# PSUM banks and transpose order at the head of a transformer block, and the order of its last K group

## The chip, the core and the metric

The kernel runs on one core of a Trainium2 chip. The metric is the device time of one execution in microseconds. A core has TensorE (PE in the profile; PEld is its weight load), VectorE (DVE), ScalarE (ACT), GpSimd (POOL) and SyncE (SP), which here only issues transfers.

## The reference

A DiT block with adaptive layer norm, 2 x 256 tokens, width 1152, two heads of 576, all in bf16:

```python
mod = (_silu(c) @ w_mod).reshape(B, 6, 1, D)
shift_a, scale_a, gate_a, shift_m, scale_m, gate_m = [mod[:, i] for i in range(6)]
h = _layernorm(x, axis=-1) * (1 + scale_a) + shift_a
qkv = (h @ wqkv).reshape(B, N, 3, H, Dh)
# ... softmax(q k^T) v, @ wo ...
x = x + gate_a * a
h2 = _layernorm(x, axis=-1) * (1 + scale_m) + shift_m
m = _gelu(h2 @ w_fc1) @ w_fc2
return x + gate_m * m
```

## The kernel before

The kernel is written as a list of units with their reads and writes. A helper orders them, works out who must wait for whom (in PSUM by whole bank, so that a matmul into a bank waits for every reader of that bank) and emits the waits. TensorE executes its units in program order. `S.first` fixes the order of the first units of the other engines.

At the head, four tiles of 128 tokens are normalised (`xn_t`), transposed on TensorE into PSUM (`xn_T`), and scaled by 1 + scale_a on the way out (`hk`). The scale itself is built by small two-column matmuls (`sca`) whose weights arrive by transfer, three k-tiles at a time. K (`k_first`, `k_pair`) is accumulated k-tile by k-tile as the weights arrive (a k-tile is 128 of the 1152 rows that are summed over). While TensorE has nothing to do, it runs filler matmuls (`warm`), so that its clock is up when the work starts.

```python
        XB = [(4, 5, 3), (6, 2, 7)]

        def xslot(b, kt, n=256):
            return ps16(XB[b][kt // 4], (kt % 4) * 256 + (512 if kt == 8 and b == 1 else 0), n)
# ...
        def hk(kt, b, eng="dve"):
            dst = HK[:, kt, b * 256:(b + 1) * 256]
            s1 = ps32(1 if kt == 0 else 7, 2 * kt, 1) if kt % KC == 0 and b == 0 else SC1A[:, kt * 2 + b:kt * 2 + b + 1]
            src = xslot(b, kt) if kt < KC else HX[:, kt, b * 256:(b + 1) * 256]
            if eng == "act":
                act(c_act(256, 1), lambda e: e.activation(out=dst, in_=src, func=ACTF.Copy, scale=s1), [src, s1], [dst], "hk_%d_%d" % (kt, b))
                return
            dve(345 if kt < KC else 285, lambda e: e.tensor_scalar(out=dst, in0=src, scalar1=s1, scalar2=None, op0=ALU.mult),
                [src, s1], [dst], "hk_%d_%d" % (kt, b))

# ...
        KB = [(0, 1, 5, 3), (4, 2, 6)]
        ev_rr = [0]
# ...
        S.unit("pe", 30.0, "ones_f0")
        mm(ps32(1, 0, 2), IDENT, ONES[:, 0:2], True, True)
        sc_ones(1, KC)
        warm(7, "b")
        for n, behind in ((1, "bn_ln1_1_1"), (1, "aggr_ln1_1"), (2, "veps_ln1_1"), (2, "rstd_ln1_1"), (1, "bn_ln1_2_1"), (2, "bn_ln1_2_2")):
            warm(n, behind, behind)
        sca(0, 3)
        xn_T(1)
        sca(3, 6)
        xn_T(0)
        sca(6, 9)
        xn_T(2, 0, 8)
        hk(0, 0)
        sc1a(0, 1, 1)
        sc1a(1, KC)
        hk(1, 0)
        xn_T_copy(0, 4, 8, "act")
        xn_T_copy(0, 8, 9, "act")
        xn_T_copy(0, 3, 4, "act")
        hk(2, 0, "act")

        def k_first(kt):
            for i in range(4):
                k_pair((kt,), i, 0)

        k_first(0)
        k_first(1)
        xn_T(2, 8, 9)
        xn_T(3)
        xn_T_copy(1, 4, 8, "act")
        xn_T_copy(1, 8, 9, "act")
```

(`XB` are the banks of the transposes of tiles 0 and 1, then 2 and 3; `KB` those of K's pairs for the two batches.)

At the end of the K stage the shift rows (`shr`) are computed in row form, cast by DVE, transposed back (`shT`), and added to h (`hx`), from which Q is projected:

```python
        k_pair(range(KT - 2), 3, 1, bank=1)
        k_pair(range(KT - 2, KT), 3, 1, bank=1)
        for k0 in range(0, KT, 3):
            S.unit("pe", 3 * c_mm(CH) + 50.0, "shr_%d" % k0)
            for kt in range(k0, k0 + 3):
                for j, (f0, f1) in enumerate(sh_split):
                    mm(psum[32 * j:32 * j + 2, 0:(f1 - f0) * 128], ST[:, kt:18:9], WSH[:, kt, f0 * 128:f1 * 128],
                       kt == 0, kt == KT - 1, tile_position=(0, 32 * j))
        copy_on("dve", SHR[0:98, :], psum[0:98, 0:CH], CH, False, "shr_ev")
        k17(0, KC, KT)
        k17(1, 0, 1)
        S.unit("pe", KT * 27.0, "shT")
        for j, (f0, f1) in enumerate(sh_split):
            for f in range(f0, f1):
                mm(ps32(0, f * 2, 2), SHR[0:98, (f - f0) * 128:(f - f0 + 1) * 128], IDENT[0:98, 32 * j:32 * j + 2], f == 0, f == KT - 1,
                   skip_group_check=True)
        k17(1, 1, KT)
```

## Time and profile before

| | |
|---|---|
| median of 3 runs before the prediction | 244.41 us (244.25 to 244.98) |
| busy: TensorE, DVE, ACT, GpSimd | 98%, 50%, 28%, 9% |
| fillers at the head (128x512 matmuls) | 5 and 16 |
| K's first matmul, K's k-tile 2, Q's first matmul | 11.07, 13.57, 33.08 us |

To read it: busy time counts a filler like any other matmul, so 98% says that TensorE sets the end, not that it does useful work all the time. The idle time ahead of a group, in square brackets, is given with what released it. The page and its views merge instructions; where I give times to a hundredth of one instruction, they are of the records in the trace that these views are made of. Q's first matmul has no record in this trace (some matmul records are missing); its 33.08 is inferred from its neighbours. The lines themselves stand in the prediction.

### The profile page before, as it was taken

The numbers are of one execution on the slowest core, as the hardware profiler recorded it, in microseconds if no ns is written. First come the engines' busy times: TensorE is split into PE (matmuls) and PEld (weight loads), VectorE is DVE, ScalarE is ACT, GpSimd is POOL, SyncE is SP. The second block draws the span as 40 slices with busy tenths as digits, with TensorE's granted clock in tenths as the row PEclk, the third lists the DMA queues.
The fourth block names the chain that finished last, engine by engine and source line by source line (L and its number), as shares of the span: only waits on it lengthen the run. The fifth ranks groups of instructions, "written<-read, shape, count | busy, mean of one in ns | idle before, by whom it ended". The sixth has DMA issues, their size and how long they took to land.

```text
span 243.1 us, 4000 instructions
## 1 busy us (share of the span) xinstructions
PE 238.2 (98%) x1719; PEld 146.4 (60%) x1728; DVE 120.5 (50%) x219; ACT 67.0 (28%) x136; POOL 21.2 (9%) x39
## 2 busy tenths in 40 slices
PE   7999999999999999999999999999999999999995
PEld 2688854556667666898444444444666566665664
DVE  3833379596988799689999500000022211111112
ACT  4820440355424106973233222223000000000000
POOL 1500000000021186400000000020000000000000
PEclk9999999999999999999999999999999999999999
DMA  6999999999995999999953498002000000000000
GB/s 233 330 362 388 390 391 390 397 413 406 392 357 168 355 389 391 391 311 392 311 170 78 145 329 302 0 24 77 0 16 19 16 16 19 16 16 29 22 16 18
DMA packets 31196, 51.58 MB, mean 212 GB/s; under 512 B 1479, under 2 KB 16843, under 8 KB 31179
## 3 DMA queue, kind: packets, MB, share of 16 engines
q1 hardware_dynamic: 30736, 50.14, 58.3%
q0 software_dynamic: 416, 1.19, 1.5%
q8 instruction: 13, 0.21, 0.4%
q14 instruction: 4, 0.03, 0.0%
q10 hardware_dynamic: 27, 0.00, 0.0%
HBM read 50.14 MB, written 1.19 MB: 211 GB/s over the span
## 4 chain that ended last, share of the span: by engine, by line
PE 98%; DVE 1%; issue 0%; POOL 0%; POOLq 0%
PE psum L688 96%; PE psum L691 2%; DVE arena L972 0%; POOL arena L713 0%; DVE arena L1296 0%; DVE arena L1297 0%; POOL arena L712 0%; DVE arena L963 0%; POOL arena L717 0%; POOLq L1358 0%
## 5 line engine op out<-in xcount | busy, mean ns | idle before, releaser
L688 PE MATMUL psum<-arena 128*128 128x384 bf16 (+9 forms) x1630 | 235.0, 310 | 2.0 <-POOL arena L717 1.4
L688 PEld LDWEIGHTS psum<-arena 128*128 128x128 bf16 (+1 forms) x1639 | 141.2, 97 | 92.0 <-issue 4.1
L1088 DVE SCALAR_TENSOR_TENSOR arena<-arena 128x1152 f32<-128x1152 bf16 x32 | 44.7, 1414 | 0.6
L1296 DVE TENSOR_TENSOR arena<-psum,arena 128x384 f32<-128x384 f32 (+2 forms) x13 | 6.8, 527 | 68.3 <-PE psum L688 68.3
L1204 ACT ACTIVATE arena<-psum 128x512 bf16<-128x512 f32 (+1 forms) x44 | 22.4, 520 | 42.7 <-PE psum L688 42.7
L683 ACT ACTIVATE arena<-psum 128x512 bf16<-128x512 f32 (+6 forms) x38 | 19.9, 546 | 41.0 <-PE psum L688 39.6
L685 DVE CAST arena<-psum 128x512 bf16<-128x512 f32 (+3 forms) x13 | 8.2, 640 | 9.5 <-PE psum L688 9.5
L669 POOL DMA_DIRECT2D dit_scratch<-arena x3 | 1.8, 617 | 116.2 <-DVE arena L685 59.4
L1172 POOL TENSOR_TENSOR arena<-arena 128x384 f32<-128x384 f32 x12 | 10.9, 912 | 10.6 <-DVE arena L1171 9.0
L1115 DVE CAST arena<-psum 72x32 bf16<-72x32 f32 x1 | 0.2, 186 | 21.3 <-PE psum L688 21.3
L741 DVE BATCH_NORM_STATS2 arena<-arena 128x6 f32<-128x384 f32 (+1 forms) x18 | 9.4, 550 | 0.3 <-DMA arena<-in_x_dram 0.2
L1177 ACT ACTIVATE arena<-arena 128x1152 bf16<-128x1152 f32 x4 | 5.3, 1344 | 11.5 <-DVE arena L1176 11.5
L1171 DVE TENSOR_TENSOR arena<-psum,arena 128x384 f32<-128x384 f32 x12 | 6.5, 549 | 1.4 <-PE psum L688 1.4
L1297 DVE TENSOR_TENSOR arena<-arena 128x384 bf16<-128x384 f32 (+2 forms) x13 | 6.8, 527 | 0.5
L691 PE MATMUL psum<-arena 128*128 128x128 bf16 (+1 forms) x89 | 7.1, 219 | 0.0
L691 PEld LDWEIGHTS psum<-arena 128*128 128x128 bf16 (+1 forms) x89 | 5.7, 98 | 1.8 <-DMA arena<-in_c_dram 0.8
L1194 ACT ACTIVATE arena<-psum,arena 128x128 bf16<-128x128 bf16 x16 | 6.0, 456 | 1.3 <-PE psum L691 0.7
L1191 DVE TENSOR_SCALAR arena<-psum,arena 128x128 bf16<-128x128 bf16 x20 | 5.4, 335 | 1.9 <-PE psum L691 1.9
L1092 DVE STREAM_TRANSPOSE arena<-arena 128x1152 f32<-128x1152 f32 x4 | 5.5, 1370 | 0.0
L1095 DVE TENSOR_REDUCE arena<-arena 128x36 f32<-128x1152 f32 x4 | 5.4, 1346 | 0.0
L1018 ACT ACTIVATE arena<-psum,arena 128x256 bf16<-128x256 f32 x8 | 3.7, 472 | 1.3 <-PE psum L688 0.9
L745 POOL TENSOR_TENSOR arena<-arena 128x1 f32<-128x1 f32 x6 | 3.7, 619 | 1.6 <-DVE arena L744 1.6
(48 smaller groups left out, 44.8 us busy)
## 6 DMA issues: line engine op xcount, KB each, us to landing
arena<-in_w_fc_dram SPq DMA_DIRECT2D x9, 1152.0 KB, 7.1
arena<-in_w_fc_dram SPq DMA_DIRECT2D x4, 2592.0 KB, 17.2
arena<-in_w_mod_dram SPq DMA_DIRECT2D x18, 288.0 KB, 8.7
arena<-in_wqkv_dram SPq DMA_DIRECT2D x18, 288.0 KB, 8.7
arena<-in_w_mod_dram SPq DMA_DIRECT2D x3, 1728.0 KB, 20.1
arena<-in_w_mod_dram SPq DMA_DIRECT2D x3, 864.0 KB, 12.0
arena<-in_wqkv_dram SPq DMA_DIRECT2D x1, 2592.0 KB, 17.4
arena<-in_wo_dram SPq DMA_DIRECT2D x1, 2592.0 KB, 24.7
```

Source lines behind the costliest of these rows:

```text
L683: act(c_act(n), lambda e: e.activation(out=dst, in_=src, func=ACTF.Copy), [src], [dst], name)
L685: dve(c_dve_psum16(n) if psum16 else c_dve_psum32(n), lambda e: e.tensor_copy(dst, src), [src], [dst], name)
L688: S.instr(lambda e: e.matmul(o, lhsT=l, rhs=r, start=st, stop=sp, **kw), reads=[l, r], writes=[o])
L691: S.instr(lambda e: e.transpose(o, i_, idn), reads=[i_, idn], writes=[o])
L741: dve(550, lambda e, s=s, o=o: e.bn_stats(out=o, in_=s), [s], [o], "bn_%s_%d" % (tag, ci))
L1088: dve(1270, lambda e, w=w, s=s, acc=acc: e.scalar_tensor_tensor(out=acc, in0=w, scalar=s, in1=acc, op0=ALU.mult, op1=ALU.add), [w, s, acc] ...
L1171: dve(550, lambda e, o=o, ga=ga, x1c=x1c: e.tensor_tensor(out=x1c, in0=o, in1=ga, op=ALU.mult), [o, ga], [x1c], "wo_t1_%d_%d" % (t, ci))
L1172: S.op("pool", 930, lambda e, xs=xs, x1c=x1c: e.tensor_tensor(out=x1c, in0=x1c, in1=xs, op=ALU.add), reads=[x1c, xs], writes=[x1c], name=" ...
L1194: act(440, lambda e, o=o, dst=dst, s1=s1, s2=s2: e.activation(out=dst, in_=o, func=ACTF.Identity, scale=s1, bias=s2), [o, s1, s2], [dst], ...
L1204: act(c_act(ntok), lambda e: e.activation(out=dst, in_=o, func=ACTF.Gelu_apprx_tanh), [o], [dst], "gelu_%d_%d" % (f, tok0))
L1296: dve(c_dve_psum32(w), lambda e, o=o, gm=gm, t1=t1: e.tensor_tensor(out=t1, in0=o, in1=gm, op=ALU.mult), [o, gm], [t1], "fc2_t1_%d_%d" % ( ...
L1297: dve(c_dve_32(w), lambda e, t1=t1, x1c=x1c, ost=ost: e.tensor_tensor(out=ost, in0=t1, in1=x1c, op=ALU.add), [t1, x1c], [ost], "fc2_out_%d ...
```

## The change

The intent: let K start earlier. Tile 1 is normalised before DVE finishes tile 2's statistics; tile 0's last five transposes lie behind the last scale sums, where TensorE used to run transposes of tile 2; tiles 2 and 3 follow K's second k-tile; K's first batch gets banks that ACT isn't still reading; and two small groups change places at the end of the K stage. The diff, in full but for one hunk of DVE, ACT and GpSimd order lists that follows from the rest:

```diff
--- before.py
+++ after.py
@@ -722,7 +722,7 @@
         for i in range(5):
             S.unit("pe", 430.0, "warm_a%d" % i)
             mm(ps32(5), IDENT, Q4B, True, True)
-        CT_PS = ps16(6, 0, 18)
+        CT_PS = ps16(4, 0, 18)
         S.unit("pe", 100, "c_T")
         tr(CT_PS, CSB[0:18, :], IDENT[0:18, 0:18])
         act(200, lambda e: e.activation(out=TH, in_=CT_PS, func=ACTF.Tanh, scale=0.5), [CT_PS], [TH], "c_tanh")
@@ -764,7 +764,7 @@
                 [xt, m, rs], [xn], "xn_%d" % t)
 
 
-        XB = [(4, 5, 3), (6, 2, 7)]
+        XB = [(4, 5, 3), (3, 5, 7)]
 
         def xslot(b, kt, n=256):
             return ps16(XB[b][kt // 4], (kt % 4) * 256 + (512 if kt == 8 and b == 1 else 0), n)
@@ -799,7 +799,7 @@
 
         def hk(kt, b, eng="dve"):
             dst = HK[:, kt, b * 256:(b + 1) * 256]
-            s1 = ps32(1 if kt == 0 else 7, 2 * kt, 1) if kt % KC == 0 and b == 0 else SC1A[:, kt * 2 + b:kt * 2 + b + 1]
+            s1 = ps32(6 if kt == 0 else 7, 2 * kt, 1) if (kt % KC == 0 or kt == 1) and b == 0 else SC1A[:, kt * 2 + b:kt * 2 + b + 1]
             src = xslot(b, kt) if kt < KC else HX[:, kt, b * 256:(b + 1) * 256]
             if eng == "act":
                 act(c_act(256, 1), lambda e: e.activation(out=dst, in_=src, func=ACTF.Copy, scale=s1), [src, s1], [dst], "hk_%d_%d" % (kt, b))
@@ -813,7 +813,7 @@
                 mm(ps32(bank, half * 256, 256), WK[:, kt, j * 128:(j + 1) * 128], HK[:, kt, b * 256:(b + 1) * 256], kt == 0 and half == 0,
                    kt == KT - 1, skip_group_check=True)
 
-        KB = [(0, 1, 5, 3), (4, 2, 6)]
+        KB = [(0, 1, 2, 6), (4, 5, 3)]
         ev_rr = [0]
 
         def k_pair(kts, i, b, bank=None):
@@ -834,7 +834,7 @@
 
         def mod_f0(kt):
             S.unit("pe", 27.0, "sca0_%d" % kt)
-            mm(ps32(1, 0, 2), WSC[:, kt, 0:P], ST[:, kt:18:9], False, kt == KT - 1, skip_group_check=True)
+            mm(ps32(6, 0, 2), WSC[:, kt, 0:P], ST[:, kt:18:9], False, kt == KT - 1, skip_group_check=True)
 
         def sca(k0, k1):
             for kt in range(k0, k1):
@@ -847,25 +847,27 @@
             mm(ps32(7, 2 * ka, 2 * (kb - ka)), IDENT, ONES[:, 2 * ka:2 * kb], True, True)
 
         S.unit("pe", 30.0, "ones_f0")
-        mm(ps32(1, 0, 2), IDENT, ONES[:, 0:2], True, True)
+        mm(ps32(6, 0, 2), IDENT, ONES[:, 0:2], True, True)
         sc_ones(1, KC)
         warm(7, "b")
-        for n, behind in ((1, "bn_ln1_1_1"), (1, "aggr_ln1_1"), (2, "veps_ln1_1"), (2, "rstd_ln1_1"), (1, "bn_ln1_2_1"), (2, "bn_ln1_2_2")):
+        for n, behind in ((1, "bn_ln1_1_1"), (1, "aggr_ln1_1"), (2, "veps_ln1_1"), (1, "rstd_ln1_1")):
             warm(n, behind, behind)
+        xn_T(1)
         sca(0, 3)
-        xn_T(1)
+        warm(1, "d")
         sca(3, 6)
-        xn_T(0)
+        warm(1, "f", "bn_ln1_2_2")
+        xn_T(0, 0, 4)
         sca(6, 9)
-        xn_T(2, 0, 8)
+        xn_T(0, 4, 9)
         hk(0, 0)
-        sc1a(0, 1, 1)
+        sc1a(0, 1, 6)
         sc1a(1, KC)
         hk(1, 0)
+        xn_T_copy(0, 8, 9, "act")
         xn_T_copy(0, 4, 8, "act")
-        xn_T_copy(0, 8, 9, "act")
+        hk(2, 0, "act")
         xn_T_copy(0, 3, 4, "act")
-        hk(2, 0, "act")
 
         def k_first(kt):
             for i in range(4):
@@ -873,8 +875,9 @@
 
         k_first(0)
         k_first(1)
-        xn_T(2, 8, 9)
-        xn_T(3)
+        xn_T(2)
+        xn_T(3, 0, 4)
+        xn_T(3, 4, 9)
         xn_T_copy(1, 4, 8, "act")
         xn_T_copy(1, 8, 9, "act")
         for kt in range(2, KC):
@@ -938,7 +941,6 @@
         sh_split = ((0, 3), (3, 5), (5, 7), (7, 9))
         SHR = sb(O_P, 768)
         k_pair(range(KT - 2), 3, 1, bank=1)
-        k_pair(range(KT - 2, KT), 3, 1, bank=1)
         for k0 in range(0, KT, 3):
             S.unit("pe", 3 * c_mm(CH) + 50.0, "shr_%d" % k0)
             for kt in range(k0, k0 + 3):
@@ -947,13 +949,14 @@
                        kt == 0, kt == KT - 1, tile_position=(0, 32 * j))
         copy_on("dve", SHR[0:98, :], psum[0:98, 0:CH], CH, False, "shr_ev")
         k17(0, KC, KT)
-        k17(1, 0, 1)
+        k17(1, 0, 2)
         S.unit("pe", KT * 27.0, "shT")
         for j, (f0, f1) in enumerate(sh_split):
             for f in range(f0, f1):
                 mm(ps32(0, f * 2, 2), SHR[0:98, (f - f0) * 128:(f - f0 + 1) * 128], IDENT[0:98, 32 * j:32 * j + 2], f == 0, f == KT - 1,
                    skip_group_check=True)
-        k17(1, 1, KT)
+        k_pair(range(KT - 2, KT), 3, 1, bank=1)
+        k17(1, 2, KT)
         for b in range(2):
             copy_on("act", QK[:, 17, b * 256:(b + 1) * 256], ps32(7, 256 * (1 - b), 256), 256, False, "qk_ev17_%d" % b)
         dma(WV, wqkv_v[:, :, 2 * D:3 * D], D * D * 2, "ld_wv", run=2304)
# ... (S.first: order lists of DVE, ACT and GpSimd)
```

More of the change, by code (lines that the diff above doesn't have):

```diff
@@ L978, in build_kernel @@
             "dve": ["zq4b", "c_half", "c_silu", "bn_ln1_1_0", "bn_ln1_1_1", "bn_ln1_1_2", "aggr_ln1_1", "veps_ln1_1", "bn_ln1_2_0",
-                    "bn_ln1_2_1", "bn_ln1_2_2", "aggr_ln1_2", "veps_ln1_2", "xn_1", "xn_0", "xn_2", "var_ln1_3", "hk_0_0", "sc1a_0", "sc1a_1", "hk_1_0",
-                    "xn_3", "hk_0_1", "hk_1_1", "hk_2_1", "xnT_cp1_3"]
+                    "bn_ln1_2_1", "xn_1", "bn_ln1_2_2", "xn_0", "aggr_ln1_2", "veps_ln1_2", "hk_0_0", "hk_1_0", "sc1a_0", "var_ln1_3", "sc1a_1",
+                    "xn_2", "xn_3", "hk_0_1", "hk_1_1", "hk_2_1", "xnT_cp1_3"]
                    + [x for kt in range(KC, KT) for b in range(2) for x in (["hk_%d_%d" % (kt, b)] + (["sc1a_%d" % kt] if kt % KC == 0 and b == 0 else []))],
-            "act": ["ld_c", "c_tanh", "sum_ln1_0", "sq_ln1_0", "sum_ln1_3", "sq_ln1_3", "xnT_cp0_4", "xnT_cp0_8", "hk_2_0", "xnT_cp0_3",
+            "act": ["ld_c", "c_tanh", "sum_ln1_0", "sq_ln1_0", "sum_ln1_3", "sq_ln1_3", "xnT_cp0_8", "xnT_cp0_4", "hk_2_0", "xnT_cp0_3",
                     "xnT_cp1_4", "xnT_cp1_8"],
-            "pool": ["ones", "ident", "nhalf", "rowpad0", "rowpad640", "mm_ln1_0", "rstd_ln1_1", "var_ln1_0", "rstd_ln1_0", "rstd_ln1_2",
-                     "mm_ln1_3", "rstd_ln1_3"],
+            "pool": ["ones", "ident", "nhalf", "rowpad0", "rowpad640", "mm_ln1_0", "rstd_ln1_1", "var_ln1_0", "rstd_ln1_0", "mm_ln1_3",
+                     "rstd_ln1_2", "rstd_ln1_3"],
         }
```

## The prediction

> **What bounds the kernel now.** I read the page's busy shares first, then its chain of work that ended last, to learn which engine sets the end.
>
> ```profile
> PE 238.2 (98%) x1719; PEld 146.4 (60%) x1728; DVE 120.5 (50%) x219; ACT 67.0 (28%) x136; POOL 21.2 (9%) x39
> ...
> PE 98%; DVE 1%; issue 0%; POOL 0%; POOLq 0%
> PE psum L688 96%; PE psum L691 2%; DVE arena L972 0%; POOL arena L713 0%; DVE arena L1296 0%; DVE arena L1297 0%; POOL arena L712 0%; DVE arena L963 0%; POOL arena L717 0%; POOLq L1358 0%
> ```
>
> The chain is TensorE from end to end. The change removes no useful matmul: all nine k-tiles of four x-tiles are still transposed, and K, shift and scale keep their matmuls. So it can gain in only two ways: fewer filler matmuls (the "warm" ones, which TensorE runs while it has nothing to do, and which the busy share counts as work), and shorter waits. The waits of TensorE in the first 36 us come next; they hardly name any:
>
> ```profile
> PE psum L688 <- POOL arena L717: 1.4, 1, 1.4
> PE psum L688 <- DVE arena L972: 0.2, 1, 0.2
> ```
>
> The 1.4 us is the start and stays. The fillers are visible only in the timeline, as 128x512 matmuls at the head:
>
> ```profile
> 6.63 1.47 DVE L741 BATCH_NORM_STATS2 arena<-arena 128x6 f32<-128x384 bf16 x3
> 6.79 0.57 POOL L745 TENSOR_TENSOR arena<-arena 128x1 f32<-128x1 f32 x1 [0.41 <-DVE arena L744]
> ...
> 8.47 1.71 DVE L762 TENSOR_SCALAR arena<-arena 128x1152 bf16<-128x1152 bf16 x3
> ...
> 8.63 0.94 POOL L745 TENSOR_TENSOR arena<-arena 128x1 f32<-128x1 f32 x1 [0.35 <-DVE arena L744]
> ...
> 9.10 0.68 PE L691 MATMUL psum<-arena 128*128 128x128 bf16 x9
> ...
> 9.61 0.38 PE L688 MATMUL psum<-arena 128*128 128x2 bf16 x9
> ...
> 9.86 0.66 PE L691 MATMUL psum<-arena 128*128 128x128 bf16 x9
> ...
> 10.36 0.38 PE L688 MATMUL psum<-arena 128*128 128x2 bf16 x9
> 10.55 1.30 ACT L683 ACTIVATE arena<-psum 128x1024 bf16<-128x1024 bf16 x2 [0.81 <-PE psum L688]
> ...
> 10.66 0.36 DVE L807 TENSOR_SCALAR arena<-psum 128x256 bf16<-128x256 bf16 x1 [0.41 <-PE psum L688]
> ...
> 11.63 0.11 PEld L688 LDWEIGHTS psum<-arena 128*128 128x128 bf16 x2 [0.23 <-ACT arena L683]
> 11.90 0.11 PEld L688 LDWEIGHTS psum<-arena 128*128 128x128 bf16 x2 [0.16 <-ACT arena L683]
> ```
>
> The reader is to see: tile 1's transposes start at 9.10, the moment DVE has normalised it (8.47 + 0.57 = 9.04); K's first matmul follows the first scaling of h (10.66 + 0.36 = 11.02, K at 11.07); and twice inside K's first k-tile a weight load waits for ACT, because K's banks 5 and 3 still hold transposes that ACT copies out. Instruction by instruction the trace has 16 fillers between 3.87 and 8.77. The last cold one starts at 6.38; from 6.81 they follow every 0.216.
>
> The second place is the end of the K stage, in the timeline from 31 us:
>
> ```profile
> 31.21 0.56 DVE L685 CAST arena<-psum 98x384 bf16<-98x384 f32 x1 [3.37 <-PE psum L688]
> 31.83 0.99 PEld L688 LDWEIGHTS psum<-arena 98*128 98x128 bf16 x17 [0.16 <-DVE arena L685]
> 32.53 1.46 DVE L972 TENSOR_SCALAR arena<-arena 128x256 bf16<-128x256 bf16 x7
> 33.06 0.76 PEld L688 LDWEIGHTS psum<-arena 128*128 128x128 bf16 x5 [0.24 <-DVE arena L972]
> ```
>
> TensorE waits for the shift rows' cast (0.05 us between matmuls), and Q's first matmul waits for the first two shifted halves of h.
>
> **What the Trainium skill says.** "TensorE: Matmul & The Clock Gate", section "Wait — 56ns, not 53.3ns?", gives N / 2.4 GHz + about 2.5 ns between warm matmuls; the trace agrees (0.0557 for a transpose of 128 columns, 0.109 for 256, 0.216 for 512, 0.0265 for the two-column scale sums), and I use the trace's. The same page, section "What's actually happening", says the array is at half clock until a window of about 3.4 us has been busy and that the window runs freely; here fillers take 0.427 until 6.81 and 0.216 after, and no run shows yet how far that moment moves. "PSUM — Partial Sum Buffer", section "PSUM bank collisions raise a hardware error", says engines must be kept apart by bank and quadrant; the kernel's waits are per bank, which is why bank numbers can matter here at all: the two waits for ACT above are for banks. "SBUF — State Buffer", section "Who interferes with whom", says VectorE's fast modes lock out GpSimd for an instruction; it fits the 0.94 us of the power on GpSimd under two normalisations, against 0.57 without.
>
> **The change at the head, step by step** (times of the timeline before).
> 1. DVE now normalises tile 1 before the third statistics of tile 2. Statistics start every 0.46: 6.63, 7.095, so the normalisation starts at 7.555 (its rstd is ready on GpSimd at 7.36), ends at 8.13, and TensorE can take tile 1 at 8.18, the wake-up being 0.05 as before.
> 2. Only 12 fillers precede it. The eighth starts at 6.81 and the twelfth ends at 7.91: TensorE now idles 0.27 until 8.18. Nine transposes: 0.51, to 8.69.
> 3. Scale sums 0 to 2: 9 x 0.027 = 0.24, to 8.94 (weights landed at 7.81). A filler: 9.15. Sums 3 to 5: 9.39 (landed 8.69). A filler: 9.61. Both fillers are cheap, for the sums of 6 to 8 need weights that landed at 9.57.
> 4. Four transposes of tile 0: 0.22, to 9.83. DVE had tile 0 ready at 9.08 (8.50 + 0.58).
> 5. Sums 6 to 8: 0.24, to 10.08. The third of them completes feature tile 0's scale; it starts at 9.89 and lasts 0.16, so DVE, reacting 0.05 to 0.08 later, starts the first scaled half at 10.10 to 10.14, ends it 0.36 later, and K may start at 10.51 to 10.55.
> 6. In that latency lie the last five transposes of tile 0: 0.28, to 10.36. This is the heart of the change: before, eight transposes of tile 2 lay there. TensorE waits 0.15 to 0.19. K's first weights landed at 10.32.
> 7. K's k-tile 0 uses banks 0, 1, 2 and 6, which no copy of ACT holds: eight matmuls without the two waits (0.12 + 0.05 before). k-tile 1 follows at 11.40 (weights at 11.05; its scale is now read from PSUM, so scaled by 10.75). It ends at 12.28.
> 8. Eighteen transposes of tiles 2 and 3: 1.00, to 13.28. Bank 5 is free of ACT's copy at about 11.85; tile 3 is normalised at about 12.2 and wanted at 12.78.
> So k-tile 2 starts at about 13.28 where the timeline before has it at 13.57: **0.29 gained**, 0.25 to 0.30. Cross-check by what vanishes and appears: two fillers x 0.216 = 0.43 and waits of 0.09 + 0.03 + 0.12 + 0.05 = 0.29 go; 0.27 and about 0.17 come; 0.28.
>
> **The change at K's end.** Four matmuls of K's last group move from before the shift rows to behind the shift transposes, and one of the last K group moves before them. The cast is covered by 8 instead of 7 matmuls of 0.109: its 0.05 goes. The addition of shift to h is covered by 4 + 7 = 11 instead of 8 matmuls, 0.33 more; the wait at 33.06, 0.14 between matmul slots, goes. K's last bank is now copied out later by ACT, but Q wants that bank only at its sixth matmul, over 1.8 us after the group's end. **0.19 gained.**
>
> **Does the gain survive?** The transfers in the first 50 us follow one another and don't move with TensorE, so I compared landings with needs. The last shift weights land at 29.18; they are wanted at 30.26, now 0.28 + 0.44 earlier, 29.54: 0.36 left. Q's weights land every 1.5 us while Q eats one k-tile in 1.29; the last lands at 42.29 and is wanted at 43.4, now about 42.95: 0.65 left. V's land at 49.82, wanted at 52.95. Later needs lie microseconds behind their landings, and the softmax work on DVE starts from Q's evictions, so it moves along. The sum: 0.28 + 0.19 = 0.47 in the trace; rounded for the clock's phase and noise, 244.41 - 0.46 = **243.95 us**.
>
> **Rivals.** (a) The head is latency-bound elsewhere: GpSimd's rstd of tile 0 (7.72, 0.56) would now be locked out by the normalisation from 7.56 to 8.13, delaying tile 0 to about 9.5; wanted at 9.61, so for it speaks the 0.94 row, against it a margin of 0.1. If it falls through, the head's 0.28 shrinks to 0.1 and the time is 244.1. (b) The shift weights or Q's take over as the bound: their margins of 0.36 and 0.65 are the smallest; a transfer 0.4 late would return some tenths, 244.1 to 244.3. (c) The warm-up comes later than 6.81 in many runs: then more of the 16 fillers before were cold, each costing 0.21 more, and four fewer ahead of tile 1 save more; 243.6. One of the three runs before is at 244.98, which speaks for such a spread. (d) The idle 0.27 lets the clock fall back: against it, it is a twelfth of the skill's window.
>
> **Range and chances.** All steps together are worth 0.2 to 0.8 us; the three runs before spread by 0.73. I put 8 in 10 on 243.4 to 244.45. Two per cent is 4.9 us; nothing here is of that size: faster 0.01, within 0.98, slower 0.01.
>
> **What would show it.** In the profile after: tile 1's transposes at about 8.2 after a wait of 0.25 for DVE; K's first 128x256 matmul at about 10.5 released by DVE L807; no weight load waiting for ACT L683 in K's first k-tile; eighteen transposes in a row at about 12.3 and k-tile 2 at about 13.3; at the start of Q no wait for L972, Q starting near 32.6. Wrong would be: a wait for a transfer at the shift rows or in Q, K's start after 10.7, or a span shorter by under 0.2 or over 0.8.

## The result, and the profile after

| | median | runs |
|---|---|---|
| before | 244.52 us | 4 (244.25 to 244.98) |
| after | 244.09 us | 4 (243.88 to 244.43) |

The ratio is 0.9981, with a 95% interval of 0.996 to 1.0003. A ratio is the mean time of one kernel's fast runs over that of the other's in the same rounds, so it isn't quite the ratio of the medians. The gain of 0.43 us between medians is near the predicted 0.46 and inside the noise. A second set (5 runs, the experiment "again" below) gave 244.26 against 244.33, ratio 0.9988 (0.9976 to 1.0). So the times alone say: faster by 0.1 to 0.4 us, or nothing. The steps have to be read in the profile.

The profile after happens to be of the slowest of the four runs (244.43). The page's chain, engines then lines:

```profile
PE 95%; DVE 2%; DMA 2%; issue 0%
PE psum L688 93%; PE psum L691 2%; DMA arena<-in_x_dram 2%; DVE arena L741 1%; DVE arena L975 0%; DVE arena L762 0%; DVE arena L742 0%; DVE arena L1299 0%; DVE arena L1300 0%; DVE arena L966 0%; DVE arena L744 0%
```

The chain now runs back through DVE's normalisation (L762) and statistics (L741) to the transfer of x: the head hangs on x's landing, no longer on fillers. TensorE's waits in the first 36 us say the same (total, times, longest):

```profile
PE psum L688 <- POOL arena L717: 1.4, 1, 1.4
PE psum L691 <- DVE arena L762: 0.4, 1, 0.4
PE psum L688 <- DVE arena L742: 0.3, 1, 0.3
PE psum L688 <- DVE arena L741: 0.2, 1, 0.2
```

Here x landed 0.17 us later than in the profile before (first statistics at 4.94 against 4.77), and the clock was up at 4.44 instead of 6.84, so that the fillers were over early and waited for the statistics that they are tied to. The timeline of the head:

```profile
7.72 0.56 DVE L762 TENSOR_SCALAR arena<-arena 128x1152 bf16<-128x1152 bf16 x1
...
8.34 0.68 PE L691 MATMUL psum<-arena 128*128 128x128 bf16 x9 [0.36 <-DVE arena L762]
...
9.98 0.38 PE L688 MATMUL psum<-arena 128*128 128x2 bf16 x9
...
10.22 0.44 PE L691 MATMUL psum<-arena 128*128 128x128 bf16 x5
10.29 0.62 DVE L807 TENSOR_SCALAR arena<-psum 128x256 bf16<-128x256 bf16 x2 [0.64 <-PE psum L688]
...
10.76 1.66 PEld L688 LDWEIGHTS psum<-arena 128*128 128x128 bf16 x16 [0.28 <-DMA arena<-in_wqkv_dram]
10.79 1.91 PE L688 MATMUL psum<-arena 128*128 128x256 bf16 x16
...
12.53 1.17 PE L691 MATMUL psum<-arena 128*128 128x128 bf16 x18
...
13.54 1.15 PE L688 MATMUL psum<-arena 128*128 128x256 bf16 x9
```

Tile 1's transposes start on DVE's word; the five transposes lie beside DVE's first scaling; K's sixteen matmuls run without a wait for ACT; eighteen transposes follow in a row. At the end of the K stage, TensorE has no wait for a cast or for L975 (the former L972) any more; one group now covers it all:

```profile
30.28 3.60 PE L688 MATMUL psum<-arena 128*2 128x384 bf16 x32
...
30.75 0.56 DVE L685 CAST arena<-psum 98x384 bf16<-98x384 f32 x1 [2.93 <-PE psum L688]
...
32.15 1.66 DVE L975 TENSOR_SCALAR arena<-arena 128x256 bf16<-128x256 bf16 x8
```

Two lengths are the same in nearly every profile of a kernel, whatever x's landing does, and I use them below. (A profile is of one execution.) **A** is from the first statistics on DVE to the first matmul of K's k-tile 2; **C** is from there to the first score matmul (64 rows). Before: A 8.80, C 33.20 us. After: A 8.60, C 33.01. So the head gained 0.20 and the K end 0.19.

Yet the profiled span is 243.2 against 243.1: by A and C it should be 0.39 us shorter, and it is 0.07 longer. Of this 0.46, 0.17 is x's landing. The largest part is a new wait, which TensorE has at 98 us, in the first fc1 tiles (timeline, weight loads only):

```profile
98.60 0.10 PEld L688 LDWEIGHTS psum<-arena 128*128 128x128 bf16 x1 [0.15 <-DVE arena L1194]
98.86 0.10 PEld L688 LDWEIGHTS psum<-arena 128*128 128x128 bf16 x1 [0.16 <-DVE arena L1194]
99.11 0.22 PEld L688 LDWEIGHTS psum<-arena 128*128 128x128 bf16 x3 [0.16 <-DVE arena L1194]
```

With a smaller one at 93.0 it makes 0.41 us between matmul slots (a slot is the time from one matmul's start to the next one's when neither waits). From the first score matmul to the last matmul of all it is 193.74 us instead of 193.29, so 0.45 with the small slots behind it. The tail, from there to the end, was 0.17 shorter than before, which closes the sum. DVE is late at 98 us, as its chain starts with the attention gate, which is computed as a row, stored and loaded back to all partitions. Its first broadcast landed at 83.84, against 83.08 before, though TensorE had passed the gate's rows 0.22 earlier.

### The profile page after: what moved, and what is told of

It reads as the page before. It is cut to its first block, busy times and chain, and to the rows that moved or that the text cites. A ratio compares the mean times of both kernels' runs of the same rounds, so it can differ in the third digit from the quotient of the medians.

```text
span 243.2 us, 3996 instructions
## 1 busy us (share of the span) xinstructions
PE 237.5 (98%) x1717; PEld 145.8 (60%) x1726; DVE 120.1 (49%) x219; ACT 66.9 (28%) x136; POOL 21.5 (9%) x39
## 4 chain that ended last, share of the span: by engine, by line
PE 95%; DVE 2%; DMA 2%; issue 0%
PE psum L688 93%; PE psum L691 2%; DMA arena<-in_x_dram 2%; DVE arena L741 1%; DVE arena L975 0%; DVE arena L762 0%; DVE arena L742 0%; DVE arena L1299 0%; DVE arena L1300 0%; DVE arena L966 0%; DVE arena L744 0%
## 5 line engine op out<-in xcount | busy, mean ns | idle before, releaser
L688 PE MATMUL psum<-arena 128*128 128x384 bf16 (+10 forms) x1628 | 234.1, 309 | 2.6 <-POOL arena L717 1.4
L688 PEld LDWEIGHTS psum<-arena 128*128 128x128 bf16 (+2 forms) x1637 | 140.7, 97 | 91.9 <-issue 3.2
L741 DVE BATCH_NORM_STATS2 arena<-arena 128x6 f32<-128x384 f32 (+1 forms) x18 | 9.5, 549 | 0.5 <-DMA arena<-in_x_dram 0.4
L691 PEld LDWEIGHTS psum<-arena 128*128 128x128 bf16 (+1 forms) x89 | 5.7, 98 | 2.7 <-DMA arena<-in_c_dram 0.8
L807 DVE TENSOR_SCALAR arena<-arena,psum 128x256 bf16<-128x256 bf16 x2 | 0.6, 292 | 6.4 <-PE psum L688 6.4
```

The lines of the kernel that those rows point to most:

```text
L688: S.instr(lambda e: e.matmul(o, lhsT=l, rhs=r, start=st, stop=sp, **kw), reads=[l, r], writes=[o])
L691: S.instr(lambda e: e.transpose(o, i_, idn), reads=[i_, idn], writes=[o])
L741: dve(550, lambda e, s=s, o=o: e.bn_stats(out=o, in_=s), [s], [o], "bn_%s_%d" % (tag, ci))
```

## The experiments

Each was run with five rounds beside the kernel before on the same chip. Since what is to be told apart is mostly under 0.3 us and the scatter of a kernel's runs is 0.3 to 0.9 (1.6 in one set of the kernel before), the verdicts rest on A, C and single waits in the profiles; the times are a check. All gave correct results. The waits are those of TensorE between 85 and 105 us beyond the 0.11 us that every profile has there; the tail is from the last matmul's start to the end of the span.

| kernel | median us (runs) | ratio to before (95%) | A | C | gate lands | wait at 85-105 | tail |
|---|---|---|---|---|---|---|---|
| before | 244.22 / 244.27 / 244.33 (9, 12, 11) | 1 | 8.80 | 33.20 | 83.08 | 0 | 3.06 |
| after | 244.09 (4) | 0.9981 (0.996, 1.0003) | 8.60 | 33.01 | 83.84 | 0.41 | 2.90 |
| again | 244.26 (5) | 0.9988 (0.9976, 1.0) | 8.77 | 33.01 | 83.17 | 0 | 2.94 |
| head_only | 244.11 (5) | 0.9994 (0.9982, 1.0007) | 8.61 | 33.21 | 83.48 | 0 | 2.82 |
| kend_only | 244.24 (5) | 0.9997 (0.9984, 1.0011) | 8.80 | 33.01 | 83.05 | 0 | 3.15 |
| old_banks | 244.85 (5) | 1.002 (1.0007, 1.0033) | 9.44 | 33.01 | 83.43 | 0 | 3.08 |
| wait_form | 244.10 (5) | 0.9996 (0.9983, 1.0008) | 8.52 | 33.24 | 83.54 | 0.13 | 2.86 |
| whole_T | 244.17 (5) | 0.9989 (0.9977, 1.0001) | 8.88 | 33.01 | 82.94 | 0 | 2.93 |
| no_fill | 244.19 (5) | 0.9989 (0.9977, 1.0002) | 8.52 | 33.01 | 83.42 | 0.48 | 3.04 |
| wk_early | 244.16 (5) | 0.9992 (0.9979, 1.0005) | 8.61 | 33.01 | 83.48 | 0.22 | 2.82 |
| combo | 244.20 (6) | 0.9992 (0.9979, 1.0005) | 8.97 | 33.01 | 83.08 | 0 | 2.90 |
| gate_first | 243.48 (5) | 0.9962 (0.995, 0.9974) | 8.60 | 33.01 | 80.05 | 0 | 2.41 |
| gate_before | 243.74 (5) | 0.9971 (0.9959, 0.9983) | 8.80 | 33.20 | 79.92 | 0 | 2.42 |
| best | 243.17 (6) | 0.9949 (0.9937, 0.9961) | 8.45 | 33.35 | 79.92 | 0 | 2.41 |

The theory at this point: head and K end each gain 0.2 us and add; the head through the split of tile 0 and through the free banks. Rivals: a shared slack, banks that don't matter, K's start set by transfers or clock.

### head_only: the K end put back

```diff
-        k17(1, 0, 2)
+        k_pair(range(KT - 2, KT), 3, 1, bank=1)   # before shr, as before
+        k17(1, 0, 1)
```

> The changed kernel with the end of the K stage put back as before. My theory: the head and the K end are worth 0.2 and 0.19 us each and simply add. From the first statistics on DVE to the first matmul of K's k-tile 2: 8.60 us, as in the profile after (8.80 before). From there to the first score matmul (64 rows): 33.20 us, as before (33.01 after). Time about 0.2 us under the kernel before. Rival (the two parts share one slack, a later wait for weights takes the head's gain back): from k-tile 2 to the scores more than 33.3 us, the sum no shorter than before.

A 8.61, C 33.21: the head's gain is there without the other, and the waits at the shift rows' cast (0.05) and at Q's start are back. The time, 0.11 under before, is less than 0.2 but not apart from it.

### kend_only: only the K end

```diff
-        k_pair(range(KT - 2, KT), 3, 1, bank=1)
...
-        k17(1, 0, 1)
+        k17(1, 0, 2)
...
+        k_pair(range(KT - 2, KT), 3, 1, bank=1)
-        k17(1, 1, KT)
+        k17(1, 2, KT)
```

> The kernel before with only the end of the K stage changed. My theory: first statistics to k-tile 2 stays 8.80 us; k-tile 2 to the first score matmul falls from 33.20 to 33.01 us, 0.19 less; no wait of TensorE for DVE L972 at Q's start; time about 0.19 us under before. Rival (the wait at Q's start is only moved, to the bank that is copied out later): a wait for ACT inside Q's first k-tile, and 33.1 to 33.2 us.

A 8.80, C 33.01, and no wait for L972 at Q's start. The 0.19 is the K end's, and the two parts add (0.20 + 0.19 in A and C of the kernel after). In the times this 0.19 isn't seen (244.24 against 244.22); the profile's tail was 0.08 longer than before's, and the scatter of a kernel's runs is larger than the effect.

### old_banks: the new order with the old banks

```diff
-        XB = [(4, 5, 3), (3, 5, 7)]
+        XB = [(4, 5, 3), (6, 2, 7)]
-        KB = [(0, 1, 2, 6), (4, 5, 3)]
+        KB = [(0, 1, 5, 3), (4, 2, 6)]
```
(and the scale sums of feature tile 0 in bank 1, c's transpose in bank 6)

> The changed kernel with all PSUM banks as before, the new order kept. My theory: K's first k-tile again runs into banks 5 and 3 that ACT copies out, and worse than before, as the order has no transposes ahead of it: its third pair waits for the end of the 1.02 us copy, about 0.8 us. First statistics to k-tile 2: 9.4 us; time 0.8 us over the changed kernel, about 0.4 over before. Rival (the banks are incidental, the order alone makes the gain): 8.60 us, time as the changed kernel.

TensorE's weight loads between 10 and 13 us waited for ACT's copy out of bank 5:

```profile
PEld psum L688 <- ACT arena L683: 0.9, 1, 0.9
```

Between matmul slots it is 0.79 us. A is 9.44, C unchanged, and the time is 0.63 over before, the one experiment of the first set that the times alone could tell (its interval lies above 1). So order and banks belong together: the order without the banks is worse than neither. The converse, the banks without the order, can't be tried: banks 2 and 6 are free for K's first k-tile only since tile 2's transposes moved behind it.

### wait_form: which of two waits stands on the instruction

K's first weight load waits for DVE's first scaling and for the transfer of its weights. In the kernel after, DVE's wait became a separate instruction ahead of the load, and the load itself waited for the transfer, which had landed 0.29 us before (10.47). In the kernel before it was the other way round: there, DVE's count was 18 and the transfer's 16, and the helper sorts by count; moving the scaling up in DVE's order made it 16, a tie that the helper broke the other way. K started 0.147 us after DVE's end instead of 0.056.

```diff
-                for k, v in sorted(need.items(), key=lambda kv: (-kv[1], str(kv[0]))):
+                for k, v in sorted(need.items(), key=lambda kv: (-kv[1], kv[0][0] == "d", str(kv[0]))):
```

> The changed kernel, but where an instruction waits for an engine and a transfer whose counts tie, the engine's wait is emitted first. In the profile after K's first weight load waits for the transfer itself and for DVE in a separate instruction ahead of it; K starts 0.147 us after DVE's end, against 0.056 before, where the forms were the other way round. My theory: this order of two waits is the 0.09 us by which the head gained less than predicted (0.20 against 0.28). K's first matmul 0.06 us after the end of the first scaling, first statistics to k-tile 2: 8.51 us, time 0.09 us under the changed kernel. Rival (K's weights, landed at 10.47, or the clock delay K's start): 8.60 us and no change.

The timeline of K's start:

```profile
10.15 0.62 DVE L807 TENSOR_SCALAR arena<-psum 128x256 bf16<-128x256 bf16 x2 [0.65 <-PE psum L688]
10.56 0.33 PEld L688 LDWEIGHTS psum<-arena 128*128 128x128 bf16 x4 [0.21 <-DVE arena L807]
```

The load is released by DVE, and the idle slot before K fell from 0.29 to 0.20 us; A is 8.52, 0.08 less than after. That is the missing part of the head's gain. (From DVE's end to K's first matmul it is 0.056 to 0.058 us in the four profiles with DVE's wait on the load and the weights there in time, and 0.146 or 0.147 in all seven with the other form. In the profile after, the same slot names the transfer as the releaser, 0.28: a wait for two is put down to what the profile can see, and the weights were there already.) But C rose by 0.23, in the shift rows:

```profile
29.97 0.25 PEld L688 LDWEIGHTS psum<-arena 128*2 128x2 bf16 x12 [0.46 <-DMA arena<-in_w_mod_dram]
```

The last shift weights landed at 29.93 in this execution; they landed between 28.94 and 29.93 in all profiles. The margin of 0.36 us that the prediction found was thus already within the scatter of transfers: K can't gain much more from an earlier start.

### whole_T: tile 0 transposed in one piece

```diff
-        xn_T(0, 0, 4)
+        xn_T(0)
         sca(6, 9)
-        xn_T(0, 4, 9)
```

> The changed kernel with the split of tile 0 undone: all nine of its transposes ahead of the scale sums 6 to 8, nothing behind them. My theory: this split is the heart of the head's gain; the sums start five transposes (0.28 us) later, and TensorE then idles while the first scaling runs. First statistics to K's k-tile 2: 8.88 us (8.60 with the split, 8.80 before), so the head's gain is more than gone; time about 0.28 over the changed kernel. Rival (K's start is set by the landing of its first weights at 10.1 to 10.5, or by the clock): 8.6 us still.

```profile
10.12 0.38 PE L688 MATMUL psum<-arena 128*128 128x2 bf16 x9
...
10.42 0.62 DVE L807 TENSOR_SCALAR arena<-psum 128x256 bf16<-128x256 bf16 x2 [0.93 <-PE psum L688]
...
10.92 0.49 PE L688 MATMUL psum<-arena 128*128 128x256 bf16 x3 [0.43 <-DVE arena L807]
```

A is 8.88, to the hundredth. The split is worth 0.28 us; without it the new head would be slower than the old one. The time doesn't show it (244.17; the profile of this kernel had no wait at 92 to 99 us, the one after had 0.41).

### no_fill: without the last two fillers

```diff
-        warm(1, "d")
-        warm(1, "f", "bn_ln1_2_2")
```
(on top of wait_form)

> The changed kernel with the better form of the double wait, and without the two fillers between tile 1's transposes and tile 0's. My theory: the prediction called these fillers cheap, but sums 6 to 8 started 0.2 to 0.4 us after their weights landed; without the fillers K may start 0.3 earlier, until the landing of K's first weights (10.14 to 10.54) stops it: first statistics to k-tile 2 of 8.2 to 8.4 us (8.52 with the fillers). But the last shift weights land at 29.0 to 29.9 whatever TensorE does, and the wait for them grows by as much: k-tile 2 to the scores 33.3 to 33.5 us (33.01 without a wait), the sum of both no shorter than the 41.6 of the changed kernel by more than 0.15. Time as the changed kernel. Rival (fillers keep the clock up): 128x256 matmuls of 0.21 us in K's first k-tiles and a loss; or, with no bound by the weights, 0.4 under the changed kernel.

A didn't fall: 8.52, and C had no wait. K started at 10.32, 0.24 us earlier in the trace than in wait_form, but x had landed 0.25 earlier too, so for K the fillers' going gained nothing. Two landings stopped TensorE. The timeline names one: scale sums 6 to 8 waited for their weights.

```profile
9.48 0.30 PEld L688 LDWEIGHTS psum<-arena 128*128 128x128 bf16 x9 [0.25 <-DMA arena<-in_w_mod_dram]
```

They landed at 9.44 and the sums started at 9.48, 0.12 earlier than the 9.60 at which wait_form's would by estimate have started (9.85, less x's 0.25). The other landing is the one that I had expected, K's first weights. The timeline puts K's wait down to DVE, but the wait instruction ahead of K's first weight load, now the transfer's, ends at 10.26: 0.08 after these weights landed (10.18), and 0.14 after DVE's scaling (10.12). So K's weights came last, and the better wait form was, by estimate, the worse one here: K started 0.135 after their landing, where DVE alone would have allowed 10.18 (0.056 after its end). It is the same in combo (scaling 10.68, weights 10.73, K 10.87) and in best (10.22, 10.26, 10.39). The clock stayed up. The early TensorE met the gate's landing instead and waited 0.48 us at 92 to 99: what the head gained was given back there.

### wk_early and combo: K's weights issued earlier

```diff
-                    S.instrs[-1].deps.update(j for j in S.instrs if j.name == "ld_x1")
+                    S.instrs[-1].deps.update(j for j in S.instrs if j.name == "ld_x0")
```
(combo: with wait_form and no_fill)

> The changed kernel, but K's first weight load no longer waits for the second half of x to land, only for the first. It is issued at about 4.8 instead of 6.2 us. My theory: the transfer rate has a dip near 10 to 11 us (240 to 290 GB/s against 380) since the loads behind that wait were issued late; the dip goes, and every landing from K's second k-tile to the last shift weights comes 0.2 to 0.4 us earlier (29.0 to 29.9 before, 28.7 to 29.2 now). TensorE does not gain from it yet: first statistics to k-tile 2 8.60, time as the changed kernel within 0.15. Rival (the dip comes from the chip's memory or from small packets, not from the issue): the landings stay, or the scale weights land later, above 9.6, and the head loses 0.1 to 0.2.

> The three last edits together: better wait form, no two fillers, K's weights issued earlier. My theory: head and transfers both earlier, so the wait at the shift rows does not eat the head's gain: first statistics to k-tile 2 8.2 to 8.3, k-tile 2 to the scores 33.0 to 33.1, sum 41.2 to 41.4 against 41.6 of the changed kernel; time 0.3 under the changed kernel, about 0.6 under before. Rival (the shift weights stay the bound): the sum stays at 41.6 and so does the time.

Both missed in the landings; wk_early's A (8.61) and time were as forecast. The shift weights landed at 29.51 and 29.09, no earlier than elsewhere, and neither did K's first weights (10.45 and 10.73, against 10.09 to 10.54 in the others). In combo the scale weights landed later (9.99), as wk_early's rival said; TensorE waited for them twice (0.40 and 0.37 us) and A rose to 8.97. In wk_early itself they came at 9.60, inside the 9.34 to 9.64 of the other profiles. So the earlier issue brought nothing earlier; that it takes from the scale weights is seen in one profile of two and not shown.

### gate_first and gate_before: the gate's broadcast ahead of the fc1 weights

```diff
-        wfc1_load(2)
+        u = wfc1_load(2)
+        u.instrs[0].deps.update(j for j in S.instrs if j.name in ("ld_g00", "ld_g01"))
```

> The changed kernel, but the third and fourth blocks of fc1 weights are loaded only once the two broadcasts of the attention gate have landed. In all profiles so far those broadcasts are issued at 76.3 to 76.9 and land at 82.9 to 83.8 and 84.0 to 85.6, among fc1 loads that were issued at 75.5; in three of the seven profiles with the new head, after included, TensorE then waits 0.1 to 0.5 us at 92 to 99 us for DVE's scaling of the second layer norm. My theory: this late gate takes back part of the head's gain, as TensorE comes earlier and the gate does not. Broadcasts land at 78.5 to 80.5; no wait of TensorE at 92 to 99 beyond the 0.11 of every profile; time 0.1 to 0.3 us under the changed kernel. Rival (DVE's chain is late for another reason): the landing moves, the waits stay.

> The same edit on the kernel before. My theory: there TensorE comes 0.4 us later and did not wait at 92 to 99, so nothing is gained: time as before within 0.1. Rival (the late gate costs every kernel alike): 0.2 us or more under before, and the change itself has no part in it.

(The count in that text is off: of the eight profiles with the new head by then, four had the wait.)

The gate's broadcasts landed at 80.05 instead of 83.2 to 83.8 and took 3.9 us instead of 7.0 (before) and 7.7 (after) from issue to landing, by the median of the transfers between 68 and 85 us, and TensorE had no wait at 85 to 105 us ("again", without the edit, had none either). What ties that wait to the gate is its second broadcast: it landed at 84.84 to 85.58 in the four profiles with the wait, and at 84.63 or earlier in all others. But gate_before, where nothing was to be gained, fell by 0.59 under before. The rival had named such a number, but for the gate's sake. In the profile of gate_before A and C are as in the kernel before, and from the first score matmul to the last matmul both take 193.29 us; what differs is the tail, 2.42 us instead of 3.06. The transfers of the last microseconds (from 240.3 us on, in both kernels; for the queue line the columns are packets, MB and share) tell why. Before:

```profile
q14 instruction: 1, 0.01, 1.3%
...
out_dram<-arena SPq DMA_DIRECT2D x1, 80.0 KB, 1.6
out_dram<-arena SPq DMA_DIRECT2D x1, 16.0 KB, 2.0
```

gate_before:

```profile
q1 hardware_dynamic: 288, 0.10, 12.9%
...
out_dram<-arena SPq DMA_DIRECT2D x1, 80.0 KB, 1.6
out_dram<-arena SPq DMA_DIRECT2D x1, 16.0 KB, 1.5
```

In the kernel before, an 8 KB instruction fetch runs beside the last store. It starts at 241.68, after the last store is issued, and takes 0.59 us on one transfer engine. Fifteen of the store's sixteen completions are in by 2.51 us after the last matmul's start; the sixteenth comes at 3.02. In gate_before there is no fetch there, and all sixteen are in by 2.37. The packets tell how: the last eight data packets of the store start 2.21 us after the last matmul's start, just as the fetch ends (2.21), while all others were through by 2.02. In the kernel after both are at 2.07, in kend_only at 2.24. The Trainium skill says in "Runtime: NRT & Kernel Launch", section "Instruction fetch mechanics", that a sequencer fetches its instructions in blocks through a transfer queue of its own, at a cost that is mostly hidden; and in "DMA: Bandwidth & Descriptors", section "Queues, rings and completion order", that a completion on a transfer engine lands only after that engine's earlier writes, across its queues. The trace agrees with both but for "hidden": here the tail is 0.4 to 0.7 us longer, as the program's end waits for it. (And not only the completion came late, but the store's data.) The edit gave SP one more wait instruction (9 instead of 8 in the trace), and the fetch moved from 241.7 to 237.1 us, under an earlier store; that the one follows from the other is inferred. All eleven profiles without the edit have the fetch in the last two microseconds and a tail of 2.82 to 3.15; all three with it have no fetch there and 2.41 or 2.42.

So of gate_first's 0.78 us against "again" (medians of the same rounds), about 0.5 is the fetch (2.94 - 2.41), which has nothing to do with the gate. What is left, some 0.25 us, is within scatter, and the two profiles don't give it to the gate: from the first score matmul to the last matmul both take 193.29 us, against 193.74 in the profile after. So the wait cost 0.45 us in that execution and there was none in the one of "again"; how often it comes is not known. The earlier landing is shown, its worth in the times is not. (gate_first against gate_before is also a third measure of the change itself, without the late fetch: 243.48 against 243.74, again inside the scatter.) A kernel with one more SP instruction and the gate left alone would have told the two apart; it was not run, and this stays open.

### best

```diff
# wait_form + no_fill + gate_first
```

> The changed kernel with the better wait form, without the two fillers, and with the gate ahead of the fc1 loads. My theory: K starts at 10.3 to 10.6, the scores at 46.1 to 46.4 (46.55 after, 46.77 before), no wait at 92 to 99: time 243.7, 0.6 under before, 0.4 under the changed kernel. Rival (each gain only uncovers the next bound): a new wait, at the shift rows near 29.5 or later, and 244.0 to 244.1 again.

243.17 us, ratio 0.9949 (0.9937 to 0.9961): the fastest kernel, 1.2 us under before and 1.1 under "again". About 0.65 and 0.5 of these are the tail. The profile had the rival's wait too, at the shift rows:

```profile
29.90 0.25 PEld L688 LDWEIGHTS psum<-arena 128*2 128x2 bf16 x12 [0.57 <-DMA arena<-in_w_mod_dram]
```

0.33 us between slots, C 33.35: that execution got nothing from the earlier head, and the scores started at 46.49. The runs range from 242.83 to 243.73; that is 0.90, hardly wider than wait_form's 0.88, so the times don't show whether such a wait comes in every execution.

### again: the changed kernel once more

> The changed kernel unaltered, for a second profile and more times beside these. First statistics to k-tile 2: 8.60 us, k-tile 2 to the scores 33.01 us, if those two gains are the kernel's and not the profile's. The gate's landing and the wait at 92 to 99 may differ: 0 to 0.5 us. Time 0.2 to 0.4 us under before. Rival (the 8.60 depends on the clock's phase or on x's landing, which was 0.17 later in the first profile): 8.5 or 8.7.

C 33.01 again; but A 8.77 instead of 8.60. The rival was right that A isn't free of the clock: here the head gained only 0.03 of its 0.20, where the other profiles of this head with the old wait form (after, head_only, wk_early, gate_first) have 8.60 or 8.61. In this execution the clock came up at 7.55 us. Nine of the twelve fillers ahead of tile 1 were cold or half so (0.427 us), the last one ended at 8.26, and tile 1, ready at 8.08, waited for it 0.18. The fillers hold the head back when the clock is late; when it is early, as in the profile after (4.44), they wait for the statistics. The gate landed at 83.17 and TensorE didn't wait at 92 to 99.

## Why the prediction was right or wrong

The total was right: 244.09 measured, and 244.26 the second time, for 243.95 predicted, inside the range, and no 2% either way. That the medians fell by 0.43 where 0.46 was forecast is luck, though: the second set gave 0.07, and the range, 243.4 to 244.45, holds the 244.41 that it started from, so it couldn't tell a gain from none. What can be judged is the mechanism. By A and C the change was worth 0.39 of the 0.47 in the profile after (where 0.45 was lost again at 98 us), and 0.22 in "again". Two of the prediction's own signs of being wrong came in the profile after: K started at 10.79, past the 10.7 (0.17 of it is x's landing), and the span was 0.07 longer, not 0.2 to 0.8 shorter. In "again" K started at 10.70 and the span was 0.44 shorter. By its steps, with the 0.17 us of x's later landing taken off the times after:

- Step 1, tile 1's transposes at 8.18: 8.17. Right. Steps 3 to 5, the last sums at 9.83 and the first scaling at 10.10 to 10.14: 9.82 and 10.12. Right.
- Step 2's idle of 0.27: in the profile it was more (0.54 in that slot, since the clock was up early) and in "again" it was none. It is the clock's phase that decides; the start of the transposes is DVE's in the one and the fillers' in the other.
- Step 3's "both fillers are cheap" was half right: the sums behind them started 0.36 after their weights landed in the profile after, so they weren't waiting for these; but no run shows what the fillers alone cost. In no_fill K started 0.24 us earlier with x 0.25 earlier; best, with the gate's order changed too, has an A 0.08 under wait_form's. In both, K's weights landed after DVE's first scaling.
- Steps 5 and 6, K's start at 10.51 to 10.55: 10.62. This step failed, by 0.09. I had taken the wake-up from DVE to TensorE as 0.05 from the trace before; it was 0.147, since the two waits had changed places. wait_form shows it. The head's gain was 0.20 instead of 0.28.
- Step 6's "heart": right, 0.28 of 0.28 (whole_T).
- Step 7, no waits for ACT's banks: right, and the banks are needed for it (old_banks).
- Step 8, eighteen transposes in 1.00 us: right.
- K's end, 0.19: 0.19, also alone (kend_only).
- "Does the gain survive?": the margin at the shift rows was put at 0.36 and no wait came in the profile after; but in wait_form and best it did (0.23 and 0.33), so rival (b) is real as soon as more is gained. "Later needs lie microseconds behind their landings" was wrong. I had checked the weights and not the gate's broadcast, which lands at 82.9 to 83.8 whatever TensorE does. Four of the nine profiles with the new head and without the edit of the gate's order (after, wait_form, no_fill and wk_early) have a wait for what follows from it, 0.13 to 0.48 us; the two with the old head (before and kend_only) have none.
- Rival (a), GpSimd's power locked out by DVE's normalisation: it was lengthened, 0.80 us instead of 0.56, but tile 0 was ready at 9.31 (9.14 less x's lateness), 0.45 before it was wanted. It cost nothing.
- Rival (d), the clock falls back in the idle slot: it did not. After 0.54 us of idling the transposes still followed every 0.056 us.
- The reading of the skill: N / 2.4 GHz + 2.5 ns fits the trace for 128, 256 and 512 columns, but not for the two-column sums, for which it gives 3.3 ns and the trace has 26.5. The sums were reckoned with the trace's figure, so nothing rests on it.
- Rival (c), the warm-up's time: it moves a great deal, 4.44 to 7.55 us in the profiles. That it costs the kernel before more than the one after isn't shown: no profile of the kernel before had a clock later than 6.84.

## What to carry to other kernels

A gain of a few tenths of a microsecond in a two-hundred-microsecond kernel is found by lengths between fixed points of the trace, which mostly repeat to a hundredth (C is 33.01 in nine of the eleven profiles with the new K end), not by the total, in which a landing, the clock's phase or an instruction fetch at the very end move as much. When a producer's work is put where the consumer's latency was, check which of two waits stands on the instruction itself, and which of the two comes last, and ask of every later stage what doesn't move with the engine that got faster: here a row that makes a round trip through memory. And an edit that gains where your theory says it shouldn't deserves a look at the last two microseconds before it is credited to its idea.

## What the Trainium skill lacked or had wrong

- "TensorE: Matmul & The Clock Gate": nothing on two waits of one weight load. With the late wait on the load itself, the matmul starts 0.056 us after the releasing DVE instruction ends; with it in a separate instruction ahead of the load, 0.147. Where the late wait in the separate instruction was a transfer's (no_fill, combo, best), the matmul started 0.135 or 0.136 after the landing.
- "TensorE: Matmul & The Clock Gate", section "What's actually happening", gives plus or minus 0.5 us for the moment at which the clock comes up. In these profiles it was 4.44 to 7.55 us for the same kernel (after and again), a spread of 3.1 us, about one of the page's windows. The same section's note that one kernel showed 6, 11 or 14 cold matmuls is nearer: the 8 between 6 and 14, at this trace's 0.427 us, are 3.4 us, by estimate.
- "Runtime: NRT & Kernel Launch", section "Instruction fetch mechanics", calls the cost of a fetch mostly hidden. A fetch that falls beside the last store isn't: the last completion comes at 2.78 to 3.10 us after the last matmul's start instead of 2.36 to 2.37, and in the three kernels with one more instruction on SP it fell elsewhere.
- "DMA: Bandwidth & Descriptors" has no number for a small row that is broadcast through software descriptors while weights stream: 7.0 to 7.7 us from issue to landing among fc1 loads, 3.9 with two of these loads held back.
